# Later release of a load, smaller pieces, earlier stores and an earlier scaling in a retention and feed-forward kernel

## The chip, the cores and the metric

The kernel runs on one core of one Trainium2 chip. The metric is the device time of one execution in microseconds (us). All times of the kernel before come from three timed runs and one profiled execution.

## What is computed

Retention (a linear attention with decay) over 8 batches, 8 heads, 576 positions and a head size of 64, followed by a feed-forward part whose activation is h - tanh(h). All of it is float32.

```
scores = scale * np.matmul(q, k.transpose(0, 1, 3, 2))
Dmat = np.where(rel >= 0, gamma[:, None, None] ** rel[None, :, :], 0.0)
ret = scores * Dmat[None, :, :, :]
attn = np.matmul(ret, v)
x = attn.transpose(0, 2, 1, 3).reshape(B * S, H * D)   # 4608 x 512
h = x @ w_in                                           # 512 x 2048
out = (h - np.tanh(h)) @ w_out                         # 2048 x 512
```

## The kernel before, in words

**Tiling.** The 576 positions are cut into 9 chunks of 64. A chunk of all 8 batches is one block of 512 columns, and the work goes chunk by chunk. The hidden size 2048 is cut into 16 pieces `f` of 128. Each matmul of the feed-forward part is made three times, because every float32 number is split into a high word (which the fast float32r format holds) and a low word (the rest): high by high, high by low and low by high. `gh`/`gl`/`gs` are the words of the activation g, `xhv`/`xlv` those of x.

**Attention by turns.** Within a chunk the scores are computed directly; everything earlier comes in through a running `state` (k times v, summed over the chunks). The decay is folded into q (a table per chunk, `qtab`, multiplied in by `scale_q`, L252, on VectorE) and into v (`scale_v`, L257, on ScalarE). A *turn* m is one call of `attend`: two batches of one chunk. It issues the scores of turn m + 1, the output of turn m and the new state, 128 small matmuls in all, then what VectorE and ScalarE make of the output. An even turn belongs to the first chunk of a pair of chunks, an odd turn to the second.

**Two kinds of stages.** From chunk 3 on the chunks go in pairs. `stage_b(n, m0)` has 16 steps `f`; each calls `mm2(n, f)`, 12 matmuls of 128x512 that add piece f to the output of chunk n. In every even step a turn runs ahead of mm2, so eight turns fill one stage b and give x of the next two chunks. `stage_a` then computes the hidden layer of these two chunks with seven products in place of eight (Strassen's scheme over two chunks and two pieces). It needs seven *variants* of the weights: three are the raw words of `w_in`, four are sums of its blocks. They lie in DRAM (`wvar`), are stored there earlier, and are read back in slots of four variants (`load_slot`, tile `ws`, L897). g of the second chunk goes to DRAM (`spill`) and is fetched again (`fetch`, tile `s`, L470) in the next stage b. Stage b runs for n = 2, 4, 6 with turns, and for n = 8 without.

**What comes ahead of the stages.** The first part loads the weights and computes the hidden layer of chunks 0 and 1. Then 32 *late* steps (`for k, (n, f) in enumerate(late)`) make mm2 for chunks 1 and 0. In these, the loop's last lines store the raw words (`raw_words`, 24 stores of 256 KB, L693), and `sums` computes and stores the other variants (L724). In each late step g of a later piece is fetched (L470), passed through tanh (`resume`, L475 and L476) and split into words (L482, L483).

**The order of the work.** Each engine runs its instructions in the order in which the code issues them (`in_order`). All the bulk transfers here are issued on SP's queue, also in order, each when the tile it writes is free. `behind` adds a wait to the instruction issued last: a load so marked starts only after the named instruction. `load_turn(m, 0)` loads q and k of a turn (tile `qk`), at the end of `attend(m - 3)`. `load_turn(m, 1, middle)` loads its v and k rows (tile `vr`, the second portion) in an odd step, behind the instruction `middle`. `load_tables` reads the decay tables of two chunks (tile `work`).

**In stage b of before**, an odd step issues the second portion first, behind the last matmul of the even step's mm2, then `fetch_on` (the load of g for step f + 4), the tables, and only then its own mm2. In stage b of n = 2 the first three slots of variants are loaded too, in halves of 512 KB at the steps in `halves_at`.

Of the kernel before, what the change touches and what calls it, by code (L numbers as in the profile page):

```python
# [20 lines left out]
NF = DF // P  # L21
NCC = DM // P
C = 64
NC = S // C
# [47 lines left out]
def retention_ffn(ctx: ExitStack, tc: tile.TileContext, ins, out, spill, wvar):  # L72
# [264 lines left out]
    def add_state(j, new, n=2):  # L337
        st = state[:, j % B : j % B + n]
        nc.vector.tensor_tensor(st, new, st, op=ALU.add)
# [128 lines left out]
    def fetch(n, f):  # L468
        fetched[n, f] = pool.tile([P, BLK], F32, tag="g", bufs=3, name=f"s{n}_{f}")
        nc.sync.dma_start(fetched[n, f], spill[n, f])  # L470
# [7 lines left out]
    def words(n, f):  # L478
        g = fetched.pop((n, f))
        gh = pool.tile([P, BLK], F32R, tag="gh", name=f"gh{n}_{f}")  # L480
        gl = pool.tile([P, BLK], F32R, tag="gl", name=f"gl{n}_{f}")
        nc.scalar.copy(gh, g)  # L482
        nc.vector.tensor_tensor(gl, g, gh.bitcast(F32), op=ALU.subtract)  # L483
        gs[n, f] = (gh, gl)

    def mm2(n, f):
        first, final = (turn[0], turn[-1]) if n == 1 else (0, NF - 1)
        if f == first:
            ops[n] = [psp.tile([P, DM], F32, tag=f"o{t}", bufs=1, name=f"o{n}_{t}") for t in range(4)]
        if f != final:  # L490
            order = [(f, t, k) for k in range(3) for t in range(4)]
        elif n < NC - 1:
            order = [(f, t, k) for t in range(4) for k in range(3)]
        else:

            groups = [(0, 0), (0, 1), (1, 0), (1, 1), (0, 2), (1, 2), (0, 3), (1, 3)]
            order = [(f - 1 + s, t, k) for s, t in groups for k in range(3)]
        for f_, t, k in order:
            g, a = [(gs[n, f_][0], 0), (gs[n, f_][0], 1), (gs[n, f_][1], 0)][k]
            nc.tensor.matmul(  # L500
                ops[n][t], g[:, t * P : (t + 1) * P], wout[f_][:, a, :],
                start=(f_ == first and k == 0), stop=(f_ == final and k == 2),
            )
            if f_ == final and k == 2:
                (store_last if n == NC - 1 else store)(n, t)

    def store(n, t):
        o = ops[n][t]
# [181 lines left out]
    def raw_words(f, v, k):  # L690

        j, w = f // 2, win[f].bitcast(F32)
        nc.sync.dma_start(wvar[:, NV * j + v], w[:, k].rearrange("p s m -> p (s m)"))  # L693
# [42 lines left out]
    for k, (n, f) in enumerate(late):  # L736
        if k in (3, 16, 29):
            follow, scale = entry3(first + (0, 2, 5)[(3, 16, 29).index(k)], rest)
        if 0 < k < len(late) - 1:
            words(*late[k + 1])  # L740
        if k < len(late) - 2:
            resume(*late[k + 2])
        if k + 4 < len(late):
            fetch(*late[k + 4])
        if k in (3, 16, 29):

            follow()
        if k in (6, 19):
            scale()
        if k in (7, 20):  # L750
            load_part(rest[0], 0)
        if k in (10, 23):
            prep(rest.pop(), 0)
        for _ in range(2 if k < 4 else 1):
            step()
        for _ in range((k > 5) + (19 < k < 26)):
            next(summed)
        if k < len(late) - 1:
            mm2(n, f)
        for _ in range(2 if 4 <= k < 9 else k in (9, 10, 11, 12, 13, 14, 19, 21, 22, 23, 24, 25, 26, 27)):  # L760
            raw_words(*raws.pop(0))


# [3 lines left out]
    def load_tables(c):  # L767

        both = work[:, 2].rearrange("p (n i s) -> p n i s", n=2, i=4)
        nc.sync.dma_start(both, qtab_d[c - 1 : c + 1].rearrange("n p i s -> p n i s"))  # L770
        for u in range(2):
            qtabs[c + u] = both[:, u]

    tables = []
# [25 lines left out]
    def prep_turn(m, t):  # L800
        if m >= len(turns) or (m, t) in prepared:
            return
        prepared.add((m, t))
        (scale_q, scale_v)[t](turns[m])
# [12 lines left out]
    def put(v, b, src, sub):  # L817

        hi, lo = [x[:, :, b * C : (b + 2) * C].rearrange("p i (u t) -> p u i t", u=2) for x in xv[v]]
        if sub == 0:  # L820
            nc.scalar.copy(hi, src)
        else:
            nc.vector.tensor_tensor(lo, src, hi.bitcast(F32), op=ALU.subtract)  # L823
# [3 lines left out]
    def attend(m, between):  # L827

        j = turns[m]
        c, b = divmod(j, B)  # L830
        first, states = (c - FIRST) % 2 == 0, c < NC - 1
        if first and b == 0:
            new_xv()
        o = bank(f"own{j}", "own")
        outs, same = pair(m_out, j, o), []
        if states:
            new = bank(f"new{j}", "new")
            same += pair(m_state, j, new)
        more = m + 1 < len(turns)
        if more:  # L840
            sc = bank(f"s{turns[m + 1]}", "h")
            same = pair(m_score, turns[m + 1], sc) + same
        run(same, outs)
        if more:
            after_score(turns[m + 1], sc, 2)
        if first:
            a = pool.tile([P, 2, 4, C], F32, tag="cv", bufs=4, name=f"xa{j}")
            kept[b] = a
            put(0, b, o[:, :, 0:2], 0)
            put(5, b, o[:, :, 2:4], 0)  # L850
            nc.scalar.copy(a, o)
            if states:
                add_state(j, new)
            between()
            put(0, b, a[:, :, 0:2], 1)
            put(5, b, a[:, :, 2:4], 1)
        else:
            a = kept.pop(b)
            t13 = pool.tile([P, 2, 2, 2, C], F32, tag="cv", bufs=4, name=f"t13_{j}")
            t24 = pool.tile([P, 2, 2, 2, C], F32, tag="cv", bufs=4, name=f"t24_{j}")  # L860
            t1, t3, t2, t4 = t13[:, 0], t13[:, 1], t24[:, 0], t24[:, 1]
            own = pool.tile([P, 2, 4, C], F32, tag="cv", bufs=4, name=f"xb{j}")
            nc.scalar.copy(own, o)
            put(4, b, o[:, :, 2:4], 0)
            nc.vector.tensor_tensor(t3, own[:, :, 2:4], own[:, :, 0:2], op=ALU.subtract)
            nc.vector.tensor_tensor(t1, own[:, :, 0:2], a[:, :, 0:2], op=ALU.subtract)
            nc.vector.tensor_tensor(t2, t3, a[:, :, 0:2], op=ALU.add)
            nc.vector.tensor_tensor(t4, a[:, :, 2:4], t2, op=ALU.subtract)
            if states:
                add_state(j, new)  # L870
            put(3, b, t3, 0)
            put(2, b, t1, 0)
            between()
            put(1, b, t2, 0)
            put(6, b, t4, 0)
            put(2, b, t1, 1)
            put(1, b, t2, 1)
            put(3, b, t3, 1)
            put(4, b, own[:, :, 2:4], 1)
            put(6, b, t4, 1)  # L880
        prep_turn(m + 2, 0)
        prep_turn(m + 1, 1)
        load_turn(m + 3, 0)

# [4 lines left out]
    def load_slot(n, part=None):  # L889

        if n >= per * ((NC - FIRST) // 2):
            return
        if n not in slots:
            slots[n] = pool.tile([P, 4, 2, 2, P], F32R, tag=("xh0", "xh1", "xl0")[n % 3], bufs=1, name=f"ws{n}")
        at = slice(0, 4) if part is None else slice(2 * part, 2 * part + 2)
        to = slots[n].bitcast(F32).rearrange("p v s c m -> p v (s c m)")[:, at]
        nc.sync.dma_start(to, wvar[:, 4 * (n % per) + at.start : 4 * (n % per) + at.stop])  # L897

# [91 lines left out]
        for f in range(2):  # L990
            split(nb, f, fetched.pop((nb, f)), False)

    halves_at = (0, 2, 4, 8, 10, 12)

    def fetch_on(n, f):
        if f < NF:
            fetch(n, f)

    def stage_b(n, m0):

        fetch(n, 3)
        for f in range(NF):
            def ahead():
                if f + 2 < NF:
                    split(n, f + 2, fetched.pop((n, f + 2)), f % 3 == 0)

            if n < NC - 1 and f % 2 == 0:
                attend(m0 + f // 2, ahead)
            else:
                ahead()  # L1010
            if n < NC - 1 and f % 2 == 1:
                load_turn(m0 + f // 2 + 2, 1, middle)
            fetch_on(n, f + 4)
            if tables and f % 2 == 1:
                load_tables(tables.pop())
            if n == 2 and f in halves_at:
                load_slot(*divmod(halves_at.index(f), 2))
            if (n, f) != (NC - 1, NF - 2):
                mm2(n, f)
                middle = tc.nc.cur_bb.bb.instructions[-1].name  # L1020


    for f in range(NF):
# [83 lines left out]
```

## Time and profile before

| | |
|---|---|
| median of three runs (lowest, highest) | 867.67 us (866.09, 869.36) |
| the profiled execution | 867.57 us |
| its span, from first to last instruction | 865.8 us |
| mean granted TensorE clock | 0.998 |
| TensorE matmuls busy | 846.3 us, 98% |
| VectorE busy | 483.1 us, 56% |
| ScalarE busy | 365.6 us, 42% |
| packets of the main DMA queue | 69472, 172.57 MB, 59.7% of 16 engines |
| packets of the TensorE instruction queue | 60, 0.98 MB |

The stages, by the chain of waits: stage b of chunk 2 from about 261 to 330 us, of chunk 4 from 450 to 515, of chunk 6 from 636 to 697, of chunk 8 from 817; a stage a of some 120 us lies between two of them. The 32 late steps run from about 120 to 217. In the profile PE is TensorE, PEld its weight loads, DVE VectorE, ACT ScalarE, and SPq the queue of SyncE. A row of waits reads "who waited, at which line, for whom". "issue" is time in which an engine waited for nothing that the profile shows.

### The profile page before, as it was taken

The numbers are of one execution on the slowest core, as the hardware profiler recorded it, in microseconds if no ns is written. First come the engines' busy times: TensorE is split into PE (matmuls) and PEld (weight loads), VectorE is DVE, ScalarE is ACT, GpSimd is POOL, SyncE is SP. The second block draws the span as 40 slices with busy tenths as digits, with TensorE's granted clock in tenths as the row PEclk, the third lists the DMA queues.
The fourth block names the chain that finished last, engine by engine and source line by source line (L and its number), as shares of the span: only waits on it lengthen the run. The fifth ranks groups of instructions, "written<-read, shape, count | busy, mean of one in ns | idle before, by whom it ended". The sixth has DMA issues, their size and how long they took to land.

```text
span 865.8 us, 18571 instructions
## 1 busy us (share of the span) xinstructions
PE 846.3 (98%) x7701; PEld 697.6 (81%) x7702; DVE 483.1 (56%) x821; ACT 365.6 (42%) x725; POOL 73.8 (9%) x63
## 2 busy tenths in 40 slices
PE   7999999999999799999999899999999999999997
PEld 6788888878888688888888788888888888888886
DVE  5989877867567556434346665343456554343321
ACT  4887764544335334323234543232345433232321
POOL 0001001010000001212110002121200012121100
PEclk9999999999999999999999999999999999999999
DMA  9976957876688576534476565444576355352432
GB/s 319 373 241 221 364 161 267 273 256 208 218 278 314 182 258 219 176 141 175 140 219 222 177 192 206 159 158 152 180 238 201 110 170 189 127 189 79 136 108 73
DMA packets 70084, 174.67 MB, mean 202 GB/s; under 512 B 7536, under 2 KB 8944, under 8 KB 65008
## 3 DMA queue, kind: packets, MB, share of 16 engines
q1 hardware_dynamic: 69472, 172.57, 59.7%
q8 instruction: 60, 0.98, 0.4%
q10 hardware_dynamic: 528, 0.92, 0.3%
q14 instruction: 24, 0.20, 0.1%
HBM read 124.70 MB, written 48.76 MB: 200 GB/s over the span
## 4 chain that ended last, share of the span: by engine, by line
PE 88%; DVE 5%; DMA 3%; issue 2%; ACT 2%; SPq 0%; ACTq 0%; DVEq 0%
PE o L500 25%; PE o L938 15%; PE h L445 15%; PE pnew L907 7%; PE pv L907 7%; PE pown L907 4%; PE py L907 4%; PE pz L907 4%; PE s L297 3%; PE own L297 3%; PE new L297 2%; DMA s<-spill_dram 2%; DVE xlv L823 1%; DMA rwi<-in_w_in_dram 1%; DMA a<-in_first_dram 1%
## 5 line engine op out<-in xcount | busy, mean ns | idle before, releaser
L500 PE MATMUL o<-wo,gh 128*128 128x512 f32 x608 | 156.6, 394 | 3.8 <-issue 2.3
L500 PEld LDWEIGHTS o<-wo,gh 128*128 128x128 f32 x608 | 112.2, 188 | 29.6 <-issue 2.8
L957 ACT ACTIVATE th<-c 128x512 f32<-128x512 f32 x72 | 45.5, 632 | 147.3 <-DVE c L971 97.4
L961 POOL TENSOR_TENSOR c<-c,th 128x512 f32<-128x512 f32 x48 | 61.9, 1293 | 530.3 <-ACT th L957 529.1
L445 PE MATMUL h<-xh,wi 128*128 128x512 f32 x384 | 97.5, 392 | 1.1 <-ACT wi L152 0.6
L445 PEld LDWEIGHTS h<-xh,wi 128*128 128x128 f32 x384 | 71.4, 188 | 16.9 <-ACT wi L152 1.1
L500 PE MATMUL o<-wo,gl 128*128 128x512 f32 x304 | 84.2, 389 | 0.0
L938 PE MATMUL o<-wo,gs 128*128 128x512 f32 x288 | 70.6, 389 | 0.0
L500 PEld LDWEIGHTS o<-wo,gl 128*128 128x128 f32 x304 | 57.1, 188 | 12.0
L938 PEld LDWEIGHTS o<-wo,gs 128*128 128x128 f32 x288 | 54.1, 188 | 11.2
L500 PE MATMUL o<-wo,gs 128*128 128x512 f32 x240 | 60.3, 399 | 0.0
L907 PE MATMUL pnew<-xhv,ws 128*128 128x512 f32 x192 | 59.5, 391 | 0.3
L907 PE MATMUL pv<-xhv,ws 128*128 128x512 f32 x192 | 59.1, 389 | 0.0
L297 PE MATMUL own<-qk,vr 64*64 64x64 f32 x928 | 56.5, 219 | 2.3 <-issue 2.3
L297 PE MATMUL own<-qk,state 64*64 64x64 f32 x928 | 57.5, 221 | 0.0
L967 DVE TENSOR_TENSOR work<-pown,work 128x512 f32<-128x512 f32 x24 | 16.6, 690 | 66.2 <-PE pown L907 66.2
L500 PEld LDWEIGHTS o<-wo,gs 128*128 128x128 f32 x240 | 45.2, 191 | 9.9
L445 PE MATMUL h<-xl,wi 128*128 128x512 f32 x192 | 51.6, 389 | 0.0
L938 PE MATMUL o<-wo,gh 128*128 128x512 f32 x192 | 48.9, 389 | 0.0
L297 PEld LDWEIGHTS own<-qk,state 64*64 64x64 f32 x928 | 47.6, 135 | 0.4 <-issue 0.4
L297 PEld LDWEIGHTS own<-qk,vr 64*64 64x64 f32 x928 | 47.9, 136 | 0.0
L923 DVE TENSOR_TENSOR gl<-s,gh 128x512 fp32r<-128x512 f32 x44 | 30.0, 687 | 25.8 <-ACT gh L922 14.0
(147 smaller groups left out, 1508.7 us busy)
## 6 DMA issues: line engine op xcount, KB each, us to landing
ws<-wvar_dram SPq DMA_DIRECT2D x39, 1024.0 KB, 4.6
s<-spill_dram SPq DMA_DIRECT2D x94, 256.0 KB, 4.2
qk<-in_qkv_dram SPq DMA_DIRECT2D x29, 512.0 KB, 4.8
vr<-in_qkv_dram SPq DMA_DIRECT2D x29, 512.0 KB, 5.0
spill_dram<-c SPq DMA_DIRECT2D x48, 256.0 KB, 2.3
spill_dram<-g SPq DMA_DIRECT2D x36, 256.0 KB, 3.4
rwi<-in_w_in_dram SPq DMA_DIRECT2D x16, 512.0 KB, 5.6
rwo<-in_w_out_dram SPq DMA_DIRECT2D x16, 512.0 KB, 5.5
```

The costliest lines, as they stand in the source:

```text
L297: nc.tensor.matmul(out_, w, x, start=start, stop=stop)
L445: nc.tensor.matmul(hp, win[f][:, cc // 2, a, cc % 2 * P : (cc % 2 + 1) * P], x[:, cc, :], start=(k == 0), stop=(k == 3 * NCC - 1))
L500: nc.tensor.matmul(ops[n][t], g[:, t * P : (t + 1) * P], wout[f_][:, a, :], start=(f_ == first and k == 0), stop=(f_ == final and k == 2),)
L823: nc.vector.tensor_tensor(lo, src, hi.bitcast(F32), op=ALU.subtract)
L907: nc.tensor.matmul(into, w[:, a, k], x[:, k], start=start and i == 0, stop=i == len(terms) - 1, skip_group_check=not start,)
L923: nc.vector.tensor_tensor(gl, g, gh.bitcast(F32), op=ALU.subtract)
L938: nc.tensor.matmul(ops[n][t], g[:, t * P : (t + 1) * P], wout[f][:, a, :], start=(j == 0 and f == fs[0] and k == 0), stop=last_,)
L957: nc.scalar.activation(th, c, AF.Tanh)
L961: nc.gpsimd.tensor_tensor(c, c, tanh(c), op=ALU.subtract)
L967: nc.vector.tensor_tensor(u2, y, u2, op=ALU.add)
```

## The change

The change has four edits.

1. `mm2` returns the name of its seventh matmul in the usual order (third group k, tile t as `(1, 2)`), and `stage_b` issues its own mm2 ahead of the odd step's loads. The second portion of loads then waits for the seventh matmul of the odd step's own mm2, and not for the last matmul of the even step's. What stands behind it on SP's queue moves along.
2. In stage b of chunk 2, the first three slots of variants are loaded one variant at a time (256 KB) in steps 0 to 11, each right behind the fetch of g.
3. `prep_turn(m + 2, 0)`, the scaling of q, is issued right after the state sum and ahead of the split of g (`between`) and of the low words of x (`put(..., 1)`).
4. The raw words are stored two per late step in steps 0 to 8 and one per step in 9 to 14; before, two per step in 4 to 8 and one in 9 to 14, 19 and 21 to 27.

```
+            if (k, t) == (1, 2):
+                middle = tc.nc.cur_bb.bb.instructions[-1].name
...
+        return middle
...
-        for _ in range(2 if 4 <= k < 9 else k in (9, 10, 11, 12, 13, 14, 19, 21, 22, 23, 24, 25, 26, 27)):
+        for _ in range(2 if k < 9 else k < 15):
             raw_words(*raws.pop(0))
...
             if states:
                 add_state(j, new)
+            prep_turn(m + 2, 0)
...
-        prep_turn(m + 2, 0)
         prep_turn(m + 1, 1)
...
-        at = slice(0, 4) if part is None else slice(2 * part, 2 * part + 2)
+        at = slice(0, 4) if part is None else slice(part, part + 1)
...
     def fetch_on(n, f):
         if f < NF:
             fetch(n, f)
+        if n == 2 and f < NF:
+            load_slot(*divmod(f - 4, 4))
...
-            if n < NC - 1 and f % 2 == 1:
-                load_turn(m0 + f // 2 + 2, 1, middle)
-            fetch_on(n, f + 4)
-            if tables and f % 2 == 1:
-                load_tables(tables.pop())
-            if n == 2 and f in halves_at:
-                load_slot(*divmod(halves_at.index(f), 2))
-            if (n, f) != (NC - 1, NF - 2):
-                mm2(n, f)
-                middle = tc.nc.cur_bb.bb.instructions[-1].name
+            if not odd:
+                fetch_on(n, f + 4)
+            if (n, f) != (NC - 1, NF - 2):
+                middle = mm2(n, f)
+            if odd:
+                load_turn(m0 + f // 2 + 2, 1, middle)
+                fetch_on(n, f + 4)
+                if tables:
+                    load_tables(tables.pop())
```

The order on TensorE and ScalarE is unchanged. On SP, in the second turn (steps 2 and 3) and the head of the third turn of stage b of chunk 2, stood before (`qk`, `vr`: the two portions of a turn; `s`: g; `ws`: variants; `work`: tables):

```order
L791 DMA qk_3291<-in_qkv_dram 128x2x512
L470 DMA s_6_3293<-spill_dram 128x512
L897 DMA ws_3157<-wvar_dram 128x1024
L791 DMA vr_3311<-in_qkv_dram 128x2x512
L470 DMA s_7_3313<-spill_dram 128x512
L770 DMA work<-in_qtab_dram 128x2x256
L791 DMA qk_3412<-in_qkv_dram 128x2x512
```

and now, of the same place:

```order
L794 DMA qk_3292<-in_qkv_dram 128x2x512
L470 DMA s_6_3294<-spill_dram 128x512
L901 DMA ws_3157<-wvar_dram 128x512
L794 DMA vr_3324<-in_qkv_dram 128x2x512
L470 DMA s_7_3326<-spill_dram 128x512
L901 DMA ws_3157<-wvar_dram 128x512
L773 DMA work<-in_qtab_dram 128x2x256
```

The slot's piece is halved, and a second piece stands behind the g load of the odd step. On VectorE, the fourth turn of that stage (an odd turn; L309 masks the scores, L865 to L868 are the differences of the scheme, L339 the state sum, L252 the scaling of q, L923 a low word of g, L823 a low word of x) stood before:

```order
L868 TENSOR_TENSOR t_34_3519<-xa_3396,t_34_3519 128x256
L339 TENSOR_TENSOR state<-new_3451,state 128x512
L923 TENSOR_TENSOR gs<-s_8_3414,gs 128x512
L823 TENSOR_TENSOR xlv<-t_34_3518,xhv 128x2x2x64
L823 TENSOR_TENSOR xlv<-t_34_3519,xhv 128x2x2x64
L823 TENSOR_TENSOR xlv<-xb_3520,xhv 128x2x2x64
L252 TENSOR_TENSOR qk_3412<-qk_3412,work 128x2x256
L923 TENSOR_TENSOR gl_9_3562<-s_9_3436,gh_9_3561 128x512
```

and now:

```order
L872 TENSOR_TENSOR t_34_3522<-xa_3398,t_34_3522 128x256
L339 TENSOR_TENSOR state<-new_3454,state 128x512
L252 TENSOR_TENSOR qk_3414<-qk_3414,work 128x2x256
L927 TENSOR_TENSOR gs<-s_8_3416,gs 128x512
L826 TENSOR_TENSOR xlv<-t_34_3521,xhv 128x2x2x64
L826 TENSOR_TENSOR xlv<-t_34_3522,xhv 128x2x2x64
L826 TENSOR_TENSOR xlv<-xb_3523,xhv 128x2x2x64
L927 TENSOR_TENSOR gl_9_3566<-s_9_3450,gh_9_3565 128x512
```

The scaling moves ahead of the low word of g and of five low words of x (two of them repeat rows and are left out here). On SP, at the beginning of the late steps, stood before (`s`: g; `vr`, `one`: portions of turns; `wvar` from `wi`: raw words):

```order
L470 DMA s_3_1639<-spill_dram 128x512
L470 DMA s_4_1665<-spill_dram 128x512
L470 DMA s_5_1763<-spill_dram 128x512
L219 DMA vr_1765<-in_qkv_dram 128x2x512
L233 DMA one_1767<-in_qkv_dram 128x1024
```

and now:

```order
L470 DMA s_3_1641<-spill_dram 128x512
L696 DMA wvar_dram<-wi_348 128x512
L696 DMA wvar_dram<-wi_382 128x512
L470 DMA s_4_1669<-spill_dram 128x512
L696 DMA wvar_dram<-wi_382 128x512
L696 DMA wvar_dram<-wi_405 128x512
L470 DMA s_5_1769<-spill_dram 128x512
L219 DMA vr_1771<-in_qkv_dram 128x2x512
L233 DMA one_1773<-in_qkv_dram 128x1024
```

Two stores of raw words now follow each of these g loads.

More of the change, by code (lines that the diff above doesn't have):

```diff
@@ L870, in attend @@
                 add_state(j, new)
+            prep_turn(m + 2, 0)
             put(3, b, t3, 0)
@@ L991, in stage_a @@
             split(nb, f, fetched.pop((nb, f)), False)
-    halves_at = (0, 2, 4, 8, 10, 12)
     def fetch_on(n, f):
@@ L1005, in ahead @@
                     split(n, f + 2, fetched.pop((n, f + 2)), f % 3 == 0)
-            if n < NC - 1 and f % 2 == 0:
+            odd = n < NC - 1 and f % 2 == 1
+            if n < NC - 1 and not odd:
                 attend(m0 + f // 2, ahead)
```

## The prediction

> **What bounds the kernel now.** The page comes first: TensorE (PE) has work in 98% of the span. A change of order can therefore win back only the places where PE stands still or runs slowly, so I looked for those.
>
> ```profile
> span 865.8 us, 18571 instructions
> PE 846.3 (98%) x7701; PEld 697.6 (81%) x7702; DVE 483.1 (56%) x821; ACT 365.6 (42%) x725; POOL 73.8 (9%) x63
> q8 instruction: 60, 0.98, 0.4%
> ```
>
> Next the waits of PE and of its weight loads. Each row has the total, the number of waits and the longest:
>
> ```profile
> PE new L297 <- issue: 2.4, 1, 2.4
> PE own L297 <- issue: 2.3, 1, 2.3
> PE o L500 <- issue: 2.3, 1, 2.3
> PE o L500 <- ACT gh L482: 1.4, 1, 1.4
> ...
> PEld s L297 <- DVE qk L252: 4.2, 9, 0.6
> ```
>
> "issue" means that PE waited for nothing the profile shows. The chain of waits places these stops and gives a yardstick (start, length, what; x24 are the matmuls of two steps):
>
> ```profile
> 185.83 6.85 DMA s<-spill_dram
> ...
> 263.18 5.67 PE o L500 x24
> ...
> 287.33 2.32 issue
> 289.65 5.28 PE o L500 x22
> 296.60 2.41 issue
> 299.93 6.77 PE o L500 x24
> ...
> 324.44 5.67 PE o L500 x24
> ...
> 452.26 2.96 PE o L500 x12
> ...
> 491.40 2.33 issue
> ...
> 509.94 5.67 PE o L500 x24
> ...
> 637.72 5.67 PE o L500 x24
> 645.42 5.67 PE o L500 x24
> ...
> 691.58 5.67 PE o L500 x24
> ```
>
> These are three stages with eight turns each, a turn being one attention part of 2.0 us and two steps of 12 matmuls. In the third, first to eighth turn are 691.58 - 637.72 = 53.86 us apart, 7.69 a turn, with no stop. In the first they are 324.44 - 263.18 = 61.26 apart, 7.40 more; in the second 509.94 - 452.26 = 57.68, 3.82 more. So 11.22 us is lost there. The stops are 2.32 + 2.41 + 2.33 = 7.06 of it; 4.16 is the small waits at the head of an attention part (for q scaled on VectorE, L252) and a stretch of slow clock after the second stop (6.77 instead of 5.67 us).
>
> What are the stops? The counts between them tell (busy time and number by engine; granted clock, share of the DMA engines, GB/s last):
>
> ```profile
> 289.65:296.60 6.95, 6.95 (x126) 5.69 (x127) 3.90 (x9) 1.86 (x6) 0.00 (x0) 1.00 0.55 163
> 299.01:491.40 192.39, 191.84 (x1903) 158.32 (x1903) 96.62 (x167) 71.65 (x153) 20.66 (x16) 0.99 0.59 194
> 483.90:485.00 1.10, 1.10 (x7) 0.92 (x6) 0.69 (x1) 1.02 (x4) 0.00 (x0) 1.00 0.00 0
> 485.00:491.20 6.20, 6.20 (x132) 5.14 (x131) 3.07 (x6) 2.43 (x7) 0.00 (x0) 1.00 0.82 254
> 491.20:493.80 2.60, 0.27 (x20) 0.14 (x13) 0.23 (x1) 0.00 (x0) 0.00 (x0) 1.00 0.04 9
> 651.00:658.70 7.70, 7.70 (x153) 6.40 (x152) 4.40 (x8) 3.33 (x9) 0.00 (x0) 1.00 0.67 204
> 120.00:134.00 14.00, 14.00 (x182) 11.60 (x181) 12.11 (x20) 7.71 (x14) 0.00 (x0) 1.00 0.20 59
> 134.00:156.00 22.00, 22.00 (x98) 18.01 (x97) 15.11 (x24) 10.65 (x18) 3.66 (x4) 1.00 0.94 312
> ```
>
> Between the first and second stop PE has 126 + 127 = 253 instructions, between the second and third 1903 + 1903 = 3806 = 15 times 253.7. The whole program has 7701 + 7702 = 15,403 for 60 packets of the instruction queue, 257 each. I read the stops as PE at the end of a block of code, about 254 plus a few uncounted waits, whose successor is not there. An attention part is 128 matmuls and 128 weight loads in 2.0 us, so one turn can use up a block in hardly more than that; the steps use 48 in 5.67 us. The third stop ends a 6.2 us run of bulk transfers, in which the code came no earlier; the stop then lasts 2.3 us in an empty DMA (share 0.04).
>
> [...]
>
> **The change part by part.** No matmul or vector operation is added; the DMA bytes are the same.
>
> *The vr load is released later.* Its release was the last matmul of the even step; it is now the seventh of the odd step, 7 x 5.67/24 = 1.65 us later. The rows of before, of SyncE and VectorE:
>
> ```profile
> 483.98 0.38 SPq L791 DMA_DIRECT2D qk<-in_qkv_dram  x1
> ...
> 486.93 0.38 SPq L791 DMA_DIRECT2D vr<-in_qkv_dram  x1
> ```
>
> ```profile
> 469.72 0.69 DVE L923 TENSOR_TENSOR gl<-s,gh 128x512 fp32r<-128x512 f32 x1 [1.08 <-ACT gh L922]
> ...
> 471.00 0.69 DVE L252 TENSOR_TENSOR qk<-qk,work 128x512 f32<-128x512 f32 x1
> ...
> 478.50 0.68 DVE L923 TENSOR_TENSOR gs<-s,gs 128x512 fp32r<-128x512 f32 x1
> ...
> 480.77 0.68 DVE L252 TENSOR_TENSOR qk<-qk,work 128x512 f32<-128x512 f32 x1
> ```
>
> A turn moves 512 + 256 KB twice, 1.57 MB, which is 6.2 us at 254 GB/s: the whole row from 485.0. The first half flows 1.0 us after its issue (nothing moves until 485.0) and needs 2.5 us (at 312 GB/s) to 3.1 (at 254), so it ends 3.5 to 4.1 us after its issue. The second was issued 2.95 after the first, flowed from 3.95 on, and there was no hole. Now it is issued at 4.60 and flows from 5.6: a hole of 1.5 to 2.1 us in each turn, ahead of the next attention part, for the next block of code. What stands behind the vr load on SP's queue is the g load of the odd step and at times the tables, 1.65 us later as well. The vr load lands after 5.0 us (page), 4.60 + 5.0 = 9.6 after the end of its turn's attention part; ScalarE scales it for the attention part that begins at 5.67 + 7.69 = 13.4, and the scaling takes 1.3. So 2.5 us are spare, and I cost this at nothing. What is paid beyond that is the slower rival.
>
> ```profile
> qk<-in_qkv_dram SPq DMA_DIRECT2D x29, 512.0 KB, 4.8
> vr<-in_qkv_dram SPq DMA_DIRECT2D x29, 512.0 KB, 5.0
> ...
> work<-in_qtab_dram SPq DMA_DIRECT2D x3, 256.0 KB, 5.2
> ```
>
> *One variant per step.* Six loads of 512 KB in steps 0, 2, 4, 8, 10, 12 become twelve of 256 KB in steps 0 to 11. The halves of a turn are now 1024 KB each: 3.4 to 4.1 us, so the hole shrinks to 0.5 to 1.2 us in the first stage's first six turns. The fourth turn, which had none of these loads, now has two. They are wanted only in the next stage. Cost in itself: nothing; its sign hangs on that hole.
>
> *q scaled earlier.* In odd turns the scaling takes the place of gs and the five low words behind it: 480.77 - 478.50 = 2.27 us earlier; in even turns 471.00 - 469.72 = 1.28. It ended at 481.45, and the next attention part starts right after; it now ends by 479.2, while PE is in its steps. The qk load (4.8 us, issued a turn before) is there. Behind it gs or gl and the low words come 0.68 us later; they are for a step two further on (over 5 us) and for the next stage. Where a table load is on its way, VectorE now waits: after 1.65 + 5.2 us instead of 5.2, against a scaling 1.28 earlier, at most some 2 us, covered by the same step. The small waits should go. The third stage shows a turn without them, but its odd turns have no state sum (0.68 us of VectorE), so I keep back a quarter of the 4.16, 1.0 us.
>
> *Raw words in steps 0 to 14.* Eight of 24 stores of 256 KB move from steps 19 to 27 to steps 0 to 3, where the DMA is at 59 GB/s. A step there then moves 768 KB, 2.5 us at 312 GB/s, in 12 matmuls of 0.236, 2.8 us: it fits, cost nothing; if it did not, a late g load would cost what the one at 185.83 did, 1.4 us. That one took 6.85 us to land, amid three raw stores, and made PE wait 1.44 for gh. Without the three, 0.79 MB or 2.5 us at 312 GB/s less, the load lands early enough: -1.44.
>
> The sum against the profiled execution's 867.57 (1.8 around its span; the median is 867.67): -7.06 (stops) - 4.16 + 1.0 (waits and slow clock) - 1.44 (late g load) = -11.66, so **855.9, say 856.0 us**.
>
> **The rivals.**
>
> *One stop is left.* In the first stage's second turn, the table load joins the second half: 512 + 3 x 256 = 1280 KB, 4.2 to 5.2 us from 5.6 on, which runs past the next first half (7.69 + 1.0 = 8.7). There is no hole just where the block used up at 287.33 must be fetched. For it: this stage has the most bytes. Against: the hole a turn later, and q no longer in the way. Price: 2.3 for the stop, to 3.5 with 1.1 of slow clock, so 858.3 to 859.5; two such stops 861.
>
> *The stops stay.* A block used up in 2.0 us is shorter than the 2.3 us that a stop lasted in an empty DMA, so the holes may not matter at all, and only block borders would. For it: the third stage, whose turns carry the same bytes at a share of 0.67, has no stop although its vr loads come just as early, so bytes alone do not make one. Against: the stop at 491.40 came after 6.2 us of transfers. Then only 1.44 and about half of 4.16 are won: 864.1. [...]
>
> *Slower: vr comes too late.* If the later vr load lands more than 5.0 + 2.5 = 7.5 us after its issue, each attention part waits for scaled v. At 8.5 us that is 1.0 in each of 23 turns, +23, and with all of the gain 879; the point where gain and loss meet by 0.5% is about 0.7 us too late. For it: the vr load now meets the next turn's first half. Against: 5.0 is the median of a crowded kernel.
>
> **How the numbers follow.** The forecast 0.50, one stop left 0.24, the stops stay 0.19, slower 0.07. A measurement can tell about 0.5%, 4.3 us, from no change. The first two are faster, and a quarter of the third: 0.78; the rest of the third 0.15; slower 0.07. The range goes from all of the gain and a measurement's scatter (853.8) up to the stops staying (864.5).
>
> **What would show it.** Right: no issue stop over 1 us in the two stages; turns of 7.7 us all through; no stretch of 24 matmuls longer than 5.7; a low DMA share about 4.5 us after each qk issue; no wait of PE for gh near 193. Wrong: issue stops at the same distance in instructions; PE waiting for vr scaled on ScalarE; PE waiting for gh in steps 0 to 8 of the late steps.

## The result and the profile after

The changed kernel takes 861.27 us (median of 4 runs, 860.20 to 862.16), the kernel before 867.87 beside it (866.09 to 869.36). The ratio is 0.9924 with a 95% interval of 0.9902 to 0.9946: 6.6 us or 0.76% faster. The forecast was 856.0, the range 853.8 to 864.5. The profiled execution took 861.5 us, 6.07 less than before's.

From the page of the changed kernel: PE is the bound as before, and the same 60 blocks of code are fetched.

```profile
span 859.7 us, 18580 instructions
PE 844.6 (98%) x7701; PEld 695.6 (81%) x7702; DVE 484.1 (56%) x821; ACT 365.2 (42%) x725; POOL 73.6 (9%) x63
q8 instruction: 60, 0.98, 0.5%
```

The waits of PE after (total, number, longest). Of three "issue" rows of 2.3 to 2.4 us one of 2.1 is left, and two of about half a microsecond; the wait for gh is as long as before.

```profile
PE o L500 <- issue: 2.1, 1, 2.1
PE o L500 <- ACT gh L482: 1.4, 1, 1.4
...
PE s L297 <- DVE qk L252: 0.5, 1, 0.5
...
PE new L297 <- issue: 0.5, 1, 0.5
```

And of its weight loads, 4.2 us in nine waits before:

```profile
PEld s L297 <- DVE qk L252: 1.8, 3, 0.9
```

The chain of waits after, with the same landmarks: first stage (to 321.12), second stage (448.90 to 503.45), and the end.

```profile
136.83 6.66 DMA s<-spill_dram
...
276.82 7.11 DMA work<-in_qtab_dram
...
287.58 2.13 issue
289.70 5.29 PE o L500 x22
...
297.74 5.66 PE o L500 x24
...
321.12 5.66 PE o L500 x24
...
448.90 5.67 PE o L500 x24
...
479.68 5.67 PE o L500 x24
488.03 5.71 PE o L500 x24
...
503.45 5.67 PE o L500 x24
...
800.27 10.88 PE o L942 x48
```

One row of PE's timeline gives the first stage's beginning, the even step of its first turn:

```profile
263.07 2.11 PE L500 MATMUL o<-wo,gh 128*128 128x512 f32 x8
```

Before, that row stands at 263.11: up to here, late steps included, nothing was won. First to eighth turn then take 321.05 - 263.07 = 57.98 us by the timeline, before 61.27: 3.3 won in the first stage. The second takes 503.45 - 448.90 = 54.55 against 57.68: 3.1 won. Seven turns without a stop are 7 x 7.69 = 53.83, so 4.15 and 0.72 are still lost, 4.87 of the 11.22. The last 48 matmuls begin at 800.27, before at 806.49.

What is left sits in five places. In the second stage, the turn between 479.68 and 488.03 is 8.35 instead of 7.69: a stop of 0.40 in its attention part. In the first, four: the stop of 2.13, at the very place of before's first one (22 of the two steps' 24 matmuls are behind it); 0.49 in the next attention part; before the first of these 0.51 for q, which VectorE scaled late because it waited for the tables; and the eighth turn, which begins 8.00 us behind the seventh, 0.31 late, for the second table load (issued at 311.41, landed after 6.68). VectorE's timeline, then the issues of SyncE:

```profile
283.95 0.69 DVE L252 TENSOR_TENSOR qk<-qk,work 128x512 f32<-128x512 f32 x1 [4.70 <-DMA work<-in_qtab_dram]
```

```profile
275.40 0.38 SPq L794 DMA_DIRECT2D vr<-in_qkv_dram  x1
...
276.82 0.42 SPq L773 DMA_DIRECT2D work<-in_qtab_dram  x1
...
278.61 0.38 SPq L794 DMA_DIRECT2D qk<-in_qkv_dram  x1
```

The table load stands behind the vr load, which is now released later; it landed 7.11 us after its issue (chain), at 283.93. VectorE waits for tables three times, 10.8 us in all; in the kernel before it never did.

The stops are still one block of code apart. Instructions of PE and of its weight loads between the stops of 2.13 and 0.49, and from there to the 0.40 of the second stage:

```profile
289.70:297.16 7.46, 6.97 (x127) 5.70 (x127) 4.20 (x10) 2.01 (x6) 0.00 (x0) 1.00 0.54 181
297.16:487.53 190.37, 189.79 (x1904) 156.85 (x1904) 96.68 (x167) 71.67 (x153) 20.69 (x16) 1.00 0.60 194
```

127 + 127 = 254, and 3808 = 15 x 253.9. This view leaves out the sequencer's own records (its waits); with these the trace has exactly 256 and 3840 = 15 x 256, in before and in after. So the borders are where they were; what happens at them changed.

The wait for gh went from 193.38 to 144.27. Its g load is the one at 136.83 on the chain. SyncE's issues ahead of it, in the fourth late step:

```profile
134.89 0.38 SPq L219 DMA_DIRECT2D vr<-in_qkv_dram  x1
135.33 0.46 SPq L233 DMA_DIRECT2D one<-in_qkv_dram  x1
135.84 0.90 SPq L696 DMA_DIRECT2D wvar_dram<-wi  x2
136.83 0.83 SPq L470 DMA_DIRECT2D s<-spill_dram  x1
```

Two loads of 512 KB and two raw stores of 256 KB are issued within 2 us ahead of it. It lands after 6.66 us (the median of these loads on the page is 4.1), and PE stands for 1.36:

```profile
s<-spill_dram SPq DMA_DIRECT2D x94, 256.0 KB, 4.1
...
vr<-in_qkv_dram SPq DMA_DIRECT2D x29, 512.0 KB, 4.3
```

### The profile page after: what moved, and what is told of

The parts are those of the page before. It is cut to its first block, busy times and chain, and to the rows that moved or that the text cites. A ratio compares the mean times of both kernels' runs of the same rounds, so it can differ in the third digit from the quotient of the medians.

```text
span 859.7 us, 18580 instructions
## 1 busy us (share of the span) xinstructions
PE 844.6 (98%) x7701; PEld 695.6 (81%) x7702; DVE 484.1 (56%) x821; ACT 365.2 (42%) x725; POOL 73.6 (9%) x63
## 4 chain that ended last, share of the span: by engine, by line
PE 79%; DVE 7%; DMA 7%; ACT 4%; issue 2%; SPq 0%; DVEq 0%; ACTq 0%
PE o L500 25%; PE o L942 15%; PE pnew L911 7%; PE pv L911 7%; PE h L445 7%; PE pown L911 4%; PE py L911 4%; PE pz L911 4%; DMA rwo<-in_w_out_dram 2%; PE s L297 2%; PE own L297 2%; DMA work<-in_qtab_dram 2%; PE new L297 2%; DMA s<-spill_dram 1%; DMA rwi<-in_w_in_dram 1%
## 5 line engine op out<-in xcount | busy, mean ns | idle before, releaser
L911 PEld LDWEIGHTS pnew<-xhv,ws 128*128 128x128 f32 x192 | 35.8, 188 | 8.9 <-DVE th L983 1.6
```

The lines of the kernel that those rows point to most:

```text
L911: nc.tensor.matmul(into, w[:, a, k], x[:, k], start=start and i == 0, stop=i == len(terms) - 1, skip_group_check=not start,)
```

## The experiments

All kernels are variants of the changed one unless said. Ratios are to the kernel before, beside which each was timed, with the 95% interval; "after" is 0.9924. Four theories are on trial for the stops and the waits. Transfers: a block's code comes late when bulk loads are under way while it is fetched (called A where letters are used). Border: the block before it is used up faster than code can be fetched, so only the border's place counts (B). Place: the stop belongs to its place in the program and not to a block (C). Raw words: what the earlier stores won or lost (D).

**tables_first.** The tables are issued ahead of the vr load, at the head of the odd step's issues:

```diff
             if odd:
+                if tables:
+                    load_tables(tables.pop())
                 load_turn(m0 + f // 2 + 2, 1, middle)
                 fetch_on(n, f + 4)
-                if tables:
-                    load_tables(tables.pop())
```

> The changed kernel, with the decay tables issued ahead of the second portion of loads, so that they no longer wait for TensorE. Theory A (a block of code is late when bulk transfers and the wait for q meet it): VectorE no longer waits 4.7 us for the table, the scaling of q ends before 283, and the stop of 2.1 us near 287.6 is gone or under 0.5 us; 858 to 859.5 us against 861.3. Theory B (only the place of the block's border counts, since a block is used up in 2.0 us there): the stop stays at 2.0 to 2.4 us, time within 0.7 us of the changed kernel.

Measured: 857.31 (856.76 to 862.93, 5 runs), 0.9877 (0.9841 to 0.9913). VectorE has no wait for the tables any more. The profiled execution is the longest of the five, 862.93, and has a longer stop than after:

```profile
286.69 3.50 issue
```

The other four took 856.8 to 858.4. So late q is cured by the order on the queue; the stop is in the one execution that has a profile and, by the times, not in the others. The time is better than either theory's forecast, but the profile bears out neither: the stop is longer, with q in time.

**shift16 and before_shift16.** Sixteen more PE instructions at the start, so that every border falls 16 instructions earlier in the program; once in the changed kernel, once in the one before. The added work is eight small matmuls with their weight loads in the warm-up, whose product is not used.

```diff
     busy(8, BLK // 2)
+    busy(8, 16)
```

> The changed kernel with 8 more tiny warm-up matmuls at the start, where TensorE waits for its first load anyway: 16 more instructions, so every border of a block of 256 instructions stands 16 instructions earlier in the program's work. The border that now falls 4 instructions into an attention part (the next block is then used up in about 2 us) falls 20 into it, and its block lasts some 4 us. Theories A and B, for which the stops are block borders: no stop of over 1 us at the same place of the program; stops move or go, 858.5 to 860 us. Theory C (the stops belong to a place of the program, by transfers or banks, and the 254 instructions between them are chance): the stop stays at the same step with 2.0 to 2.3 us, and the time stays at 861.3.

> The kernel before with the same 16 instructions at the start and nothing else changed. Block borders as the cause: the stops near 287.3, 296.6 and 491.4 us move or shrink, by 2 to 5 us in all, without any of the four edits: 862 to 866 us. If the transfers alone decide (theory A in its pure form: any border under a full DMA stops), the stops come at other borders and the time stays at 867 to 868. Theory C: the stops stay where they are, 867.9.

Measured: shift16 864.66 (10 runs), 0.9952 (0.9928 to 0.9976); before_shift16 868.94 (10 runs), 1.001 (0.9993 to 1.0027). The waits of PE, shift16 first:

```profile
PE h L445 <- issue: 2.6, 2, 2.1
...
PE new L297 <- issue: 2.3, 1, 2.3
...
PE own L297 <- issue: 0.8, 1, 0.8
```

```profile
PE h L445 <- issue: 3.0, 2, 2.2
PE own L297 <- issue: 2.1, 1, 2.1
PE new L297 <- issue: 1.9, 1, 1.9
PE o L500 <- issue: 1.6, 2, 1.3
```

The stop of 2.13 was between matmuls of o; it is now inside the attention part ahead of them, before its last six matmuls (with their loads, 12 instructions; 16 earlier than in after). So it went with the border, and theory C falls. The expectation had the direction wrong: the border that stood 4 instructions into an attention part now stands 12 ahead of it, not 20 into it. But it did not shrink (2.27), though the block that ends there now begins with some of the slower matmuls of o (24 in 5.67 us, against 128 in 2.0 us of an attention part) and lasts longer; and in the shifted kernel before there are again three stops in the two stages. B in its pure form falls too: to move the border does not remove the stop. Both kernels got new stops in the first projections (h), 2.6 and 3.0 us, which after and before do not have: a border is moved for the whole program, and what one place wins another can lose. My 858.5 to 860 for shift16 was a miss; 862 to 866 for the shifted kernel before was one too, and the transfers' 867 to 868 came nearest.

**early_release.** The first edit undone: vr released by the even step's last matmul again.

```diff
-            if (n, f) != (NC - 1, NF - 2):
-                middle = mm2(n, f)
             if odd:
                 load_turn(m0 + f // 2 + 2, 1, middle)
                 fetch_on(n, f + 4)
                 if tables:
                     load_tables(tables.pop())
+            if (n, f) != (NC - 1, NF - 2):
+                mm2(n, f)
+                middle = tc.nc.cur_bb.bb.instructions[-1].name
```

> The changed kernel without its first edit: the second portion of loads released by the last matmul of the even step, as before. If the later release, the hole between two bursts, is what let the code through (theory A): issue stops of over 2 us in both stages again, 863.5 to 866. If the earlier scaling of q did it: no new stop in the second stage, within 1 us of the changed kernel.

Measured: 865.52 (10 runs), 0.996 (0.9935 to 0.9986). The waits of PE:

```profile
PE new L297 <- issue: 2.4, 1, 2.4
PE own L297 <- issue: 2.0, 1, 2.0
PE o L500 <- issue: 1.8, 1, 1.8
```

Three stops again (287.15, 295.90, 487.96), with the same count of instructions between them as in before (126 + 127, and 1903 + 1902), at borders that after has too. The code, the borders and the bytes are those of after; only the time of issue differs. The lengths are 6.2 in all against 3.0, and the time is the 863.5 to 866 of theory A. The profiles are one execution each, and the two ratios' intervals just overlap (0.9935 to 0.9946).

**late_q.** The third edit undone: q scaled behind x's low words.

```diff
-            prep_turn(m + 2, 0)
             between()
...
-            prep_turn(m + 2, 0)
             put(3, b, t3, 0)
...
+        prep_turn(m + 2, 0)
         prep_turn(m + 1, 1)
```

> The changed kernel without its third edit: q scaled behind the low words, as before. If the earlier scaling is worth what the forecast gave it (the waits at the head of an attention part, 0.13 to 0.34 us in some nine turns, and TensorE running further ahead of a block border): waits of PEld for qk at L252 back at some 4 us in 9 turns, an issue stop of over 1.5 us back in the stage of 450 to 515 us, and 863.5 to 865. If only the spacing of the loads mattered: small waits back but no new stop, 862 to 862.7.

Measured: 867.22 (10 runs), 0.9977 (0.9947 to 1.0006). Its waits, of the weight loads and of PE:

```profile
PEld s L297 <- DVE qk L252: 4.2, 9, 0.6
```

```profile
PE own L297 <- issue: 3.7, 2, 3.3
PE o L500 <- issue: 2.4, 2, 1.9
```

The nine small waits are back to the digit. The stop of over 1.5 us that I expected in the second stage did not come (0.49 and 0.40 there); in its place the third stage has one of 3.26 at 649.75, which neither kernel has, and the time is beyond the 865 of the forecast. Of the four edits this one, taken away alone, costs most: 0.53%, 4.6 us.

**halves and raws_as_before.** The second edit undone (six loads of 512 KB), and the fourth (raw words at their old steps).

```diff
-        at = slice(0, 4) if part is None else slice(part, part + 1)
+        at = slice(0, 4) if part is None else slice(2 * part, 2 * part + 2)
...
+    halves_at = (0, 2, 4, 8, 10, 12)
...
-        if n == 2 and f < NF:
-            load_slot(*divmod(f - 4, 4))
+        if n == 2 and f - 4 in halves_at:
+            load_slot(*divmod(halves_at.index(f - 4), 2))
```

```diff
-        for _ in range(2 if k < 9 else k < 15):
+        for _ in range(2 if 4 <= k < 9 else k in (9, 10, 11, 12, 13, 14, 19, 21, 22, 23, 24, 25, 26, 27)):
```

> The changed kernel without its second edit: the variants again in halves of 512 KB at steps 0, 2, 4, 8, 10 and 12. If the pieces were worth something of themselves, by filling the bursts evenly: the stop near 287 longer or a second one over 1 us, 862 to 863.5. If they are worth nothing: 860.5 to 861.8. If their addition to the fourth turn, which had none before, keeps the stop near 287 alive: it shrinks, 859 to 860.5.

> The changed kernel with the raw words stored as before (two per late step in steps 4 to 8, one in 9 to 14, 19 and 21 to 27). Theory D (the earlier raw words only moved a late load of g from the 28th late step to the ninth): the wait for gh of 1.4 us near 144 is gone and the one near 193 is back with 1.4; within 0.8 us of the changed kernel. Theory E (the earlier raw words did what was forecast, 1.4 us, and the wait near 144 comes of something else): 1.4 us slower, 862.5 to 863.

Measured: halves 861.94 (8 runs), 0.9933 (0.9912 to 0.9954); raws_as_before 860.25 (4 runs), 0.9912 (0.9879 to 0.9946). Neither can be told from after. Without the fourth edit PE has no wait for gh near 144 and one of 0.58 near 193, not the 1.4 of theory D: of the wait near 193 the earlier raw words take away 0.58 at most, and they pay 1.36 near 144. The large stop is 1.03 in that profile, though its stage has the code of after; so much it varies.

**ws_late, combined, raws_gap, tables_gap, all_three.** Three remedies: (1) the tables first, as above; (2) the variants' twelve pieces in steps 4 to 15 instead of 0 to 11, out of the turn that carries the tables; (3) the raw words with none in the fourth step.

```diff
-        if n == 2 and f < NF:
-            load_slot(*divmod(f - 4, 4))
+        if n == 2 and f - 4 >= 4:
+            load_slot(*divmod(f - 8, 4))
```

```diff
-        for _ in range(2 if k < 9 else k < 15):
+        for _ in range(2 if k in (0, 1, 2, 4, 5, 6, 7, 8, 15) else 8 < k < 15):
```

ws_late is (2) alone; combined is (1) and (2) with two raw stores in steps 0 to 3 and one in steps 4 to 19; raws_gap is (3) alone; tables_gap is (1) and (3); all_three is all.

> The changed kernel with the twelve pieces of variants in steps 4 to 15 in place of 0 to 11, so the first two turns, one of which loads the tables, move 512 and 1024 KB less. Theory A with the table load at its core (it took 7.1 us under a full DMA, VectorE and then TensorE waited): the table lands in about 5 us, the wait for q and the stop near 287.6 are gone or under 0.5, 858 to 859.5. If the stop hangs on the border alone (a block used up in 2.0 us): it stays at about 2 us, 861.

> The changed kernel with three edits: tables ahead of the second portion, the pieces of variants in steps 4 to 15, and the raw words two per late step in steps 0 to 3 and one in 4 to 19. If the three losses left are a late table, a full DMA at one border and a late load of g: no wait of TensorE over 0.6 us between 120 and 700 us, and 855 to 857. If the late g load comes of any raw words beside the loads of attention: a wait for gh of about 1.4 us somewhere in the late steps, 857 to 858.5.

> The changed kernel with the raw words two per late step in steps 0 to 2, 4 to 8 and 15, and one in 9 to 14: only the two stores of step 3, which follow its two loads for attention, move (to step 15). If these two, ahead of the g load issued at 136.8, make that load late (6.7 us to land): no wait for gh over 0.5 us near 144 and none near 193, 859.3 to 860.2 against 861.3. If any raw words beside those loads do: the wait near 144 stays at 1 to 1.4 us and the time at 861.

> The changed kernel with the decay tables issued ahead of the second portion and the raw words as in the run with the gap at step 3. If the tables alone take the stop near 287 away where nothing disturbs (as the timed runs of the first such kernel say, 857.3, and its profile, with a stop of 3.5 us, does not): 855.5 to 857. If the stop is there in about half of the executions: 857 to 860 with a spread of over 3 us.

> The same as the run with tables and gap, and with the twelve pieces of variants in steps 4 to 15. The combined kernel before it had no stop near 287 but three waits for gh of 5.6 us in all. Without those: no wait of TensorE over 0.6 us between 120 and 700 us, 855 to 857 in every execution. If the lighter first turns add nothing to the tables: the same time as the run with tables and gap, within 0.7 us.

| kernel | us (lowest, highest, runs) | ratio (95%) |
|---|---|---|
| ws_late | 860.86 (857.90, 861.63, 4) | 0.9899 (0.9859 to 0.9939) |
| combined | 862.40 (859.95, 865.29, 10) | 0.9930 (0.9908 to 0.9951) |
| raws_gap | 862.06 (859.27, 863.22, 6) | 0.9936 (0.9908 to 0.9963) |
| tables_gap | 858.76 (856.89, 862.52, 4) | 0.9893 (0.9856 to 0.9931) |
| all_three | 858.20 (856.98, 858.77, 6) | 0.9893 (0.9868 to 0.9918) |

In ws_late the stop near 288 stays (2.10), and VectorE still waits for the tables, at most 3.2. That is what I expected if the border alone decided. combined has no stop near 287, but its raw stores make three g loads late. Its waits of PE and one of these loads on the chain, issued behind the two stores of the fourth step:

```profile
PE o L500 <- ACT gh L482: 5.6, 3, 2.6
```

```profile
137.44 7.91 DMA s<-spill_dram
```

In raws_gap, with no store there, the wait near 144 is gone (0.44 and 0.18 are left near 183 and 194), which settles its cause; but the time gains nothing against the 859.3 to 860.2 expected, and the profiled execution has a stop of 2.45 near 287 and a stretch of slow clock behind it (granted 0.50 from 290 to 293). tables_gap shows one of 2.95 in its profiled execution, the longest of four. all_three has no issue stop over 0.4 us, but one wait for gh of 0.90 near 183, and it misses the 855 to 857 expected, as combined does; it is within 0.7 us of tables_gap, so the lighter first turns add nothing that the times show. Its ratio is 0.0031 under after's, and the two intervals overlap (0.9902 to 0.9918); tables_first is lower still. I can say that they are no slower. The spread of all_three, 1.8 us in six runs, is the narrowest, but after's is 2.0 in four.

**The hole, over all profiles.** The largest stop comes right behind the attention part of the first stage's fourth turn. I took the share of the DMA engines in the quietest 2 us of the 6 us that end with that attention part. Rows of the windows view of after, combined and all_three (the share is the number before the last):

```profile
283.25:285.25 2.00, 1.49 (x36) 0.99 (x38) 1.30 (x3) 0.00 (x0) 0.00 (x0) 1.00 0.74 258
```

```profile
288.25:290.25 2.00, 2.00 (x29) 1.45 (x30) 0.21 (x1) 0.00 (x0) 0.00 (x0) 1.00 0.61 197
```

```profile
282.25:284.25 2.00, 2.00 (x58) 1.53 (x60) 0.00 (x0) 0.00 (x0) 0.00 (x0) 1.00 0.51 123
```

| kernel | quietest 2 us | start of the code's packet, us behind the attention part's start | stop there, us |
|---|---|---|---|
| early_release | 0.92 | 2.3 | 1.79 |
| halves | 0.90 | 2.8 | 2.29 |
| before | 0.86 | 2.8 | 2.32 |
| after | 0.74 | 1.8 | 2.13 |
| raws_gap | 0.73 | 2.8 | 2.45 |
| late_q | 0.71 | 2.5 | 1.94 |
| tables_first | 0.71 | 4.0 | 3.50 |
| ws_late | 0.68 | 2.4 | 2.10 |
| tables_gap | 0.65 | 3.7 | 2.95 |
| combined | 0.61 | -0.4 | none |
| raws_as_before | 0.59 | 1.2 | 1.03 |
| all_three | 0.51 | -0.3 | none |

A full DMA goes with a stop, but the share alone does not order the kernels: combined has no stop at 0.61, raws_as_before one at 0.59, and the length does not grow with the share. (The two shifted kernels have their border elsewhere.) The next column orders them nearly (a negative number is ahead of the start).

**The packets of code.** That column comes from the traces' records of the code's own queue, q8: it moves one packet of 16 KB per block (0.98 MB in 60 on the page), and the DMA view of a narrow window has a row for it when the packet starts there. In the 14 traces 53 issue stops of PE are over 0.15 us long (the first 30 us left out). Every one lies at a border of 256 instructions, to one record, and ends 1.2 to 1.6 us after the end of a packet. So the stops are late code. The packet itself takes 0.9 to 2.0 us; what varies most is its start. The second stop of the first stage shows this between early_release and after, where only the time of issue differs. The DMA ahead of the packet, then the packet's row in the next 2 us, early_release first (the 2 us ahead have no such row):

```profile
294.00:296.00 2.00, 1.90 (x105) 1.65 (x105) 0.65 (x1) 0.00 (x0) 0.00 (x0) 1.00 0.98 351
q8 instruction: 1, 0.02, 3.1%
```

```profile
292.50:294.50 2.00, 2.00 (x11) 1.65 (x10) 0.71 (x2) 0.00 (x0) 0.00 (x0) 1.00 0.04 15
q8 instruction: 1, 0.02, 4.0%
```

Under the full DMA the packet starts at 296.03, 1.9 us into the attention part, and the stop is 2.41. In the empty one it starts at 294.59, 0.3 ahead of the attention part, and the stop is 0.49. This is theory A at a single border. The 0.49 that is left, and the 0.40 of the second stage, are theory B's: their packets start 0.3 and 0.1 us ahead of the attention part in an empty DMA (share 0.04 from 292.5 to 294.5, 0.00 from 484.1 to 485.1), and PE still comes to the border too soon. The stop of 3.26 in late_q's third stage is of the first kind: the packet starts at 650.54, behind 2 us of a full DMA, and PE has stood since 649.75.

```profile
648.50:650.50 2.00, 1.25 (x86) 1.12 (x78) 1.38 (x2) 0.00 (x0) 0.00 (x0) 1.00 0.94 331
```

When a block is asked for, and how a bulk load holds its packet back, no record shows; that stays open.

## Why the prediction was right, and where not

The sign and the range were right, and so was the reading of the stops: blocks of code, late under bulk loads, and shorter or gone where a hole stands between these. But the likeliest case was not the one that came. It was the first rival, one stop left, and at the place that it named. Its price was missed too: 858.3 to 859.5 against 861.27, since it counted neither the late q nor the new wait for gh. The time fell between the forecast and the stops staying without any one case having priced it; that it lies in the range is in part luck. By the prediction's steps:

- *Stops, -7.06.* Measured: 2.13 + 0.49 + 0.40 = 3.02 left, so -4.04. The step that failed is the hole "in each turn": in the fourth turn of the first stage there was none (0.74 in the quietest 2 us), and the packet of code started 1.8 us into the attention part. The rival saw this, but not quite why: it asked for a hole where the block that ends at 287.33 is fetched. That block came in time; late is its successor's packet, two turns behind the table load. The other 0.89 is what two block borders inside attention parts cost even in an empty DMA; the prediction had put that at nothing.
- *Tables, "at most some 2 us, covered by the same step".* This failed as well. VectorE waited 4.70 and PE 0.51. I had taken the median of 5.2 for the landing of a load that I was moving into the fullest spot of the stage; it took 7.11. The scaling, too, was ready 2.7 us earlier than in before (279.25 against 281.98), not 1.28, so that even 5.2 would have left a wait of 2.8. While VectorE waited, the g load behind it was held up to 285.27 and went out just ahead of the packet. But this alone is not the cause of the stop: tables_first has no such wait, and 3.50.
- *Small waits and slow clock, -4.16 + 1.0.* Lost in the two stages besides the stops: 4.16 before, 4.87 - 3.02 = 1.85 now, so -2.31 of the 3.16 forecast. The slow stretch is gone (5.66 at 297.74 on the chain against 6.77; the granted clock is 1.00 from 299 to 301, and was 0.50 from 300 to 302 in before), and late_q shows that the small waits go by the third edit. Of what is left, 0.51 is the wait for q and 0.31 the second late table; the rest are gaps too short for a row of their own here.
- *Late g load, -1.44.* Measured: nothing. "It fits, cost nothing" counted the g load and two stores of a step, 768 KB. The fourth late step also issues 1 MB of vr and one, all ahead of the g load. raws_gap takes the stores out of that step and the wait goes. The wait near 193 did go; one as long came at 144.
- *The sum.* -4.04 - 2.31 = -6.35, measured -6.07 by the profiled executions; the remaining 0.3 I cannot place.
- *The vr load.* Right: it is no cost. vr landed in 4.3 us by the page's row (5.0 before), and PE never waited for scaled v, so the slower rival did not come.
- *The stops stay.* That rival would have the spacing of the bulk loads change nothing at a block border. early_release against after, with the same borders and bytes, speaks against it here: 6.2 us of stops against 3.0, and the packet of code at the second stop comes 1.4 us earlier (294.59 against 296.03).
- *The other blocks.* At most of the 60 block borders PE does not stop: in the profiles of before and after three borders each, behind the first 30 us, have an issue stop of over 0.15 us. These cost 7.1 us in before and 3.0 in after.

By parts, each edit taken away alone costs: q earlier 0.53% (4.6 us), vr later 0.36% (3.1 us), one variant per step 0.09% and raw words -0.12%, the last two within the error (each ratio has some 0.2 to 0.3%). The prediction gave the larger part to the vr release and the smaller to q. The runs turn that round, though the two intervals overlap. The parts add up to 0.86% against 0.76% for the whole, no difference within the error. Why the earlier q is worth more than its small waits is not shown.

## What to carry to other kernels

Count the instructions between stops that nothing in the profile explains: where they come a block of code apart, look in narrow windows for the packets of the code's queue, and space the bulk loads so that the DMA is quiet when a packet is due, here just ahead of each fast stretch (3.0 us of stops in after against 6.2 in early_release). Keep the tensor engine's small waits away from there (late_q, with nine of them again, is 4.6 us slower than after by the two ratios). One profile is one execution: look at the spread of the times before a single stop is trusted. When a load's release is moved later, go through everything that stands behind it on its queue, and price its landing by the crowded rows, not the median (7.11 us for the tables here, where the median had been 5.2). Before moving small stores to a quiet stretch, list every transfer of the very step they go to: one needed load behind them pays for all (here it landed after 6.66 us, the median being 4.1, and PE stood for 1.36).

## What the runs showed of the hardware

By the times, whether a stop comes can differ between executions of one program: tables_first took 856.8 to 858.4 in four and 862.9 in the one whose profile shows the stop of 3.50. A long stop can also be followed by a stretch at half clock, and need not be. Windows behind the stop of tables_first (the granted clock is the third number from the end), then behind that of halves, 2.29:

```profile
290.00:292.00 2.00, 1.81 (x6) 1.44 (x7) 1.72 (x6) 0.20 (x1) 0.00 (x0) 0.71 0.41 156
292.00:294.00 2.00, 2.00 (x6) 1.62 (x5) 0.00 (x0) 0.62 (x1) 0.00 (x0) 0.50 0.00 0
```

```profile
288.50:290.50 2.00, 2.00 (x9) 1.67 (x10) 2.00 (x6) 1.55 (x6) 0.00 (x0) 1.00 0.58 179
```

It is not a matter of length alone: half clock came behind 1.94 (late_q, 0.51 from 291 to 293) and 2.45 (raws_gap, 0.50 there), full clock behind 2.41 (early_release, 1.00 from 298 to 300) and 2.29. What else decides is not shown.
